# New planning costs, waiting times and an engine-pair rule in a list schedule, with two bias blocks recorded later: attention with relative bias and a mixture of experts on one NeuronCore

## The chip, the cores and the metric

The kernel runs as one program on one core of a Trainium2 chip. The metric is the device time of one execution in microseconds (us). Three runs of the kernel before took 1742.33 to 1742.76 us, with a median of 1742.48 us.

## The reference, cut to what matters

Two stages follow one another. The first is attention over 4 batches, 8 heads, 576 positions and a head size of 64; its scores get a bias from a small network over the distance of two positions. The second is a layer of 8 experts over the 2304 tokens, weighted by a matrix that eight rounds of row and column scaling have balanced.

```python
x = (log1p(abs(i - j)) / log1p(max(i, 1)))[..., None]
bias = relu(x @ w1 + b1) @ w2
attn = softmax(q @ k.T / sqrt(D) + bias) @ v
P = exp(x @ w_gate - max);  8 times: rows, then columns of P scaled
out = sum over e of P[:, e:e+1] * (relu(x @ m1[e]) @ m2[e])
```

## The kernel before, in words

Both stages are first written down as a list of nodes and then emitted in an order that a list scheduler works out when the program is built. On the chip each engine runs its instructions in just that order, and semaphores hold an instruction until its inputs are there. So the scheduler's numbers set the order of each queue and nothing else: they add no wait and take none away.

**The planner.** `Plan` (lines 44 to 171) holds the nodes. `Engine` (line 190) stands in for an engine: every call such as `vec.tensor_tensor(...)` becomes a node with a planned duration from `cost` (line 227), or for a DMA from `transfer` (line 215). `emit` (line 131) walks through planned time. For each engine it takes, of the nodes that are ready, the one with the lowest priority number and then the lowest index, which is the order in which the code recorded it (`pick`, line 144). Priority 0 is `urgent` (line 87), 2 is `later` (line 94), the rest are 1. A successor becomes ready at the planned end of a node plus an entry of `LATENCY` (line 48), or 0.17 us where the table has none. At the end all nodes are sorted by planned start and issued. The one table `LATENCY` serves both stages, while `cost` serves the attention alone: the experts' nodes carry durations that are written out by hand (`on_act`, `on_vec`, `on_pe`).

**The start.** The 16 blocks of q and k are loaded, and VectorE or ScalarE takes the largest magnitude of each. Beside that run the bias blocks: `bias_step` (line 624) issues `bias_front(i)` (line 544: one DMA of a mask for block i+3, four matmuls, four ScalarE sign operations) and `bias_back(i-1)` (line 558: two groups of 17 matmuls on TensorE and two or three VectorE operations). There are 41 blocks. Two of them follow each of eight pairs of maxima (lines 803 and 804). Then the maxima are turned into the scale of q and k by a chain under `urgent`: a reduction, a transpose on TensorE, a reduction, a small matmul, and a few VectorE operations. From block 18 on `bias_back` needs a factor that comes from this scale.

**The attention.** 16 units of two heads each go through: cutting q and k into high and low fp16 halves (`u_cut`, line 707), transposes, scores (`scores`, line 898, two PSUM buffers `s`), the maximum with the bias added (`st_max`, line 922, a VectorE instruction of 576 columns with an accumulated result, called CUSTOM_DVE_ANT_0 in the profile), the exponential with its sum (`st_exp`, line 940, ScalarE), the cut of the probabilities into a high half (`st_hi`, line 956, ScalarE) and a low half (`st_lo`, line 969, VectorE), a DMA transpose into `aT`, and the product with v (`attend`, line 983: a group of 28 matmuls into PSUM buffer `pv`, with 64 partitions each, of 256 columns in 32 groups and of 64 columns in 16). GpSimd copies halves of tiles from one set of partitions to the other. Expert 0's first products are fed in as pieces of 12 matmuls with priority 2 (`run_piece`, line 868) once the first tokens are there. All the attention's instructions have line 211 in the profile, the helper that records them.

**The experts.** Line 1191 emits the attention's plan, line 1927 that of the experts, which are seven experts of Strassen-like products on TensorE (lines 1608 and 1628 in the profile) with their evacuations on ScalarE and VectorE.

In the old `cost`, a VectorE operation is 0.12 us and 1.2 ns (SBUF) or 1.12 ns (PSUM) for each column; a ScalarE operation is 0.16 us (0.13 from PSUM), 0.03 us for each single-column operand and 0.97 ns for each column, with 0.28 us more where it accumulates.

Of the kernel before, what the change touches and what calls it, by code (L numbers as in the profile page):

```python
# [10 lines left out]
F32 = mybir.dt.float32  # L11
# [4 lines left out]
PSUM = bass.MemoryType.PSUM  # L16
# [19 lines left out]
SK = 3.0  # L36
PC = 1.305
MXP = 2
K_VEC = (1, 4, 7)
TM16 = 2.0**-16  # L40
TINY = 2.0**-100
# [2 lines left out]
class Plan:  # L44
# [1 line left out]


    LATENCY = {
        ("act", "act"): 0.13,
        ("dve", "dve"): 0.13,  # L50
        ("pool", "pool"): 0.1,
        ("pe", "pe"): 0.0,
        ("sp", "sp"): 0.0,
        ("dve", "pe"): 0.26,
        ("pe", "act"): 0.2,
        ("pe", "dve"): 0.2,
    }

    def record(self, eng, cost, fn, ins, outs, move=None):
# [71 lines left out]
    def emit(self):  # L131
        n = self.nodes
        succ, left, ready = [[] for _ in n], [len(x[3]) for x in n], [0.0] * len(n)
        for i, x in enumerate(n):
            for d in x[3]:
                succ[d].append(i)
        avail = {}
        for i, x in enumerate(n):
            if not left[i]:
                avail.setdefault(x[0], []).append(i)  # L140
        free, order, moved = {}, [], 0.0
        key = lambda i: (n[i][4], i)

        def pick(e):

            l = avail[e]
            t = max(free.get(e, 0.0), min(ready[i] for i in l))
            for i in sorted((i for i in l if ready[i] <= t), key=key):
                if not any(n[j][4] == 0 and n[i][4] and t < ready[j] < t + n[i][1] - 0.25 for j in l):
                    return t, e, i  # L150
            t = min(ready[j] for j in l if ready[j] > t)
            return t, e, min((i for i in l if ready[i] <= t), key=key)

        while any(avail.values()):
            t, e, i = min(pick(e) for e in avail if avail[e])
            avail[e].remove(i)
            order.append((t, i))
            free[e] = end = t + n[i][1]
            if n[i][6]:
                moved = max(moved, end + 0.65) + n[i][6][0]  # L160
                end = moved + 0.8
                if e == "dma":
                    free[e] = max(free[e], moved - n[i][6][1])
            for j in succ[i]:
                left[j] -= 1
                ready[j] = max(ready[j], end + n[i][5] + self.LATENCY.get((e, n[j][0]), 0.17))
                if not left[j]:
                    avail.setdefault(n[j][0], []).append(j)
        assert len(order) == len(n)
        for _, i in sorted(order):  # L170
            n[i][2]()
        self.__init__()
# [17 lines left out]
class Engine:  # L190
# [5 lines left out]
    def __getattr__(self, op):  # L196
        def call(*args, **kw):
            outs = [kw[k] for k in ("out", "accum_out") if k in kw]
            rest = list(args)
            if "out" not in kw:  # L200
                outs.insert(0, rest.pop(0))
            ins = [x for x in rest + [v for k, v in kw.items() if k not in ("out", "accum_out")] if isinstance(x, AP)]
            if op == "matmul" and not kw["start"]:
                ins.append(outs[0])
            fn = getattr(self.real, op)
            move = None
            if op.startswith("dma"):
                cost, *move = self.transfer(op, outs[0], ins[0])
            else:
                cost = self.cost(op, outs[0], ins) + (0.28 if self.name == "act" and len(outs) > 1 else 0.0)  # L210
            self.plan.record(self.name, cost, lambda: fn(*args, **kw), ins, outs, move)  # L211

        return call
# [13 lines left out]
    def cost(self, op, out, ins):  # L227

        n = max(x.free_size() for x in [out] + ins)
        columns = sum(x.free_size() == 1 for x in ins)  # L230
        if self.name == "pe":
            c = 4 if ins[0].dtype == F32 else 1
            if out.partition_size() > 64:
                return c * max(64, out.free_size()) / 2350
            return c * max(82, out.free_size()) / 3500
        if self.name == "act":
            return (0.13 if ins and ins[0].space == PSUM else 0.16) + 0.03 * columns + n * 0.00097
        if self.name == "pool":
            return 0.15 + n * 0.0016
        if op == "tensor_copy" and ins[0].dtype == out.dtype == F16:  # L240
            return 0.06 + n * 0.00027
        if n <= 2:
            return 0.08
        return 0.12 + n * (0.0012 if ins[0].space != PSUM else 0.00112)


class Places:
# [24 lines left out]
def attention_sinkhorn_moe(ctx, tc, q, k, v, w1, b1, w2, wg, m1, m2, xm, xm4, xf, sel, out):  # L272
# [12 lines left out]
    vec, act, pool, pe, sync = (  # L285
        Engine(plan, e, n)
        for e, n in ((nc.vector, "dve"), (nc.scalar, "act"), (nc.gpsimd, "pool"), (nc.tensor, "pe"), (nc.sync, "dma"))
    )
# [47 lines left out]
    def some_max(o, i, on_act):  # L336

        if on_act:
            act.activation(i, i, AF.Abs, accum_out=o)
        else:  # L340
            absmax(o, i)
# [72 lines left out]
    with ExitStack() as actx:  # L414
# [24 lines left out]
        big, hidp, scon = Places(take, 4), Places(take, 2), Places(take)  # L439
# [50 lines left out]
        def max_load(name, src, i):  # L490
            flat = src.rearrange("b h s d -> (b h s d)").rearrange("(n p x) -> n p x", p=P, x=1152)
            if name == "v":
                f = (wrk if i % 2 else bst).tile([P, 1152], F32, name="mxl", tag="aT" if i % 2 else "bt", bufs=2 + i % 2)
            else:
                f = big.tile([P, 1152], F32, name="big")
            sync.dma_start(out=f, in_=flat[i])
            mxt[name, i] = f
# [22 lines left out]
        for kind in range(1, 4):  # L520
            vec.scalar_tensor_tensor(
                out=wr,
# [8 lines left out]
            out=wa.rearrange("p g (j k) -> p (g j) k", j=4),  # L531
            in0=wr.unsqueeze(1).broadcast_to([P, 16, HID]),
            in1=selt[:, 8:24].unsqueeze(2).broadcast_to([P, 16, HID]),
            op=ALU.mult,
# [9 lines left out]
        def bias_front(i):  # L544
            t, s0, n = blk(i)
            W = 8 * n
            xm_load(i + 3)
            if i % 9 == 3 and t < 4:
                xg_load(t + 1)
            x = xq.pop(i)  # L550
            sg = hidp.tile([P, 4, 512], F16, name="sg", tag="sg")
            for g4 in range(4):
                pre = ps_l1() if g4 % 2 else psA.tile([P, 512], F32, name="pre", tag=("pv", "l2")[g4 // 2])
                pe.matmul(pre[:, :W], wa[:XR, g4], x, start=True, stop=True)
                act.activation(sg[:, g4, :W], pre[:, :W], AF.Sign)
            sgs[i] = sg
# [67 lines left out]
        def bias_step(between=()):  # L624

            i = bpos[0]
            bpos[0] += 1
            if between:
                if 0 < i <= NBLK:
                    bias_back(i - 1)  # L630
                for j, fn in enumerate(between):
                    fn()
                    if j == 0 and i < NBLK:
                        bias_front(i)
                return
            if i < NBLK:
                bias_front(i)
            if 0 < i <= NBLK:
                bias_back(i - 1)
# [12 lines left out]
            out=w1r, in0=pw[:, H : H + 2], scalar1=s_wb[:, 0:1], scalar2=2.0**-11, op0=ALU.mult, op1=ALU.mult  # L652
# [5 lines left out]
            out=w2m,  # L658
            in0=w2r.unsqueeze(2).broadcast_to([P, H, 4]),
            in1=selt[:, 4:8].unsqueeze(1).broadcast_to([P, H, 4]),  # L660
            op=ALU.mult,
# [131 lines left out]
        for n in range(8):  # L793
            for m in (2 * n, 2 * n + 1):
                nm, _, i = qk_order[m]
                some_max(mq8[:, int(nm == "k"), i : i + 1], mxt.pop((nm, i)), nm == "k" and i not in K_VEC)
                if m + 4 < 16:
                    max_load(*qk_order[m + 4])
                elif m + 4 == 16:
                    u_load(0)  # L800
                if m + 4 >= 16:
                    max_load("v", v, m - 12)
            bias_step()
            bias_step()
        with plan.urgent():
            mqk = sm([P, 2])
            vec.tensor_reduce(out=mqk, in_=mq8, axis=AX.X, op=ALU.max)
# [4 lines left out]
            out=c8, in0=u_qk[:, 0:1], scalar=0.125, in1=u_qk[:, 1:2], op0=ALU.mult, op1=ALU.mult  # L812
# [7 lines left out]
            out=g, in0=g0, scalar=s_qk[:, 0:1], in1=s_qk[:, 1:2], op0=ALU.mult, op1=ALU.mult  # L820
        )
        gbox[0] = g[:, 0:1]
        bias_step()

        def b_scale(hp):

# [21 lines left out]
            u_trans(0)  # L848
        u_load(1)
        u_cut(1)  # L850
        bias_step()
        b_scale(0)
        u_trans(1)

# [258 lines left out]
        for u in range(len(units)):  # L1113
            f = 5 * u
            g1 = 8 + 3 * u if u < 4 else f + 2
            e = 0 if u < 4 else -1
# [75 lines left out]
        vec, act, pool, pe, sync = nc.vector, nc.scalar, nc.gpsimd, nc.tensor, nc.sync  # L1192
# [289 lines left out]
    def w_max(e, w):  # L1482
        prio = 0 if e == 1 else MXP
        for i, q in enumerate(BLK):
# [413 lines left out]
    for n, (e, b) in enumerate(seq):  # L1898
        r = visit[n]
        i, at_end, leaves = (b, r % 2), n % 5 == 4, visit[n + 1 : n + 2] != [r]  # L1900
# [96 lines left out]
```

## Time and profile before

| what | value |
|---|---|
| median of three runs | 1742.48 us (1742.33 to 1742.76) |
| the profiled execution's own time | 1743.0 us |
| span of its trace | 1741.2 us |
| TensorE busy, share of the span | 1667.7 us, 96% |
| VectorE busy | 1440.8 us, 83% |
| ScalarE busy | 1070.2 us, 61% |
| GpSimd busy | 96.8 us, 6% |
| mean granted TensorE clock | 0.984 of full |

PE is TensorE's matmuls, PEld its weight loads, DVE VectorE, ACT ScalarE, POOL GpSimd and SP the queue that issues DMAs. Busy time is the union of the instructions of an engine. Two instructions that follow one another on DVE or ACT overlap a little in the trace, so what one of them costs its engine is the time from its start to the start of the next, which is less than its duration. The attention runs from 0 to about 492 us, the experts from there to the end.

### The profile page before, as it was taken

What the parts mean: (1) busy time and instruction counts of PE and PEld (TensorE: products, weight loads), DVE (VectorE), ACT (ScalarE), POOL (GpSimd) and SP (SyncE); (2) the same over time, 40 slices, a digit from 0 to 9 for tenths busy, and PEclk for the clock granted to TensorE, in tenths of its full rate; (3) what the DMA queues carried; (4) which work ended last, traced back from release to release, by engine and by line L of the source; (5) the groups of instructions that cost most, each with busy time, mean ns of one, the idle gap of its engine ahead of it and who ended that gap; (6) DMA issues with size and microseconds to landing.
All of it is one profiled execution on the core that took longest, in us unless ns stands there. A gap on an engine that the chain in (4) does not pass through costs nothing.

```text
span 1741.2 us, 40333 instructions
## 1 busy us (share of the span) xinstructions
PE 1667.7 (96%) x16596; PEld 1368.3 (79%) x16596; DVE 1440.8 (83%) x2622; ACT 1070.2 (61%) x1906; POOL 96.8 (6%) x137
## 2 busy tenths in 40 slices
PE   7887897999999999999999999999999999999998
PEld 4554564656585888888988898889888888888887
DVE  7998989898869999787878887988788878876666
ACT  7897888888857655456455545555555644443443
POOL 0102011111002310000000000000000000000000
PEclk9988898999999999999999999999999999999999
DMA  7869899999976446734664555456544743463321
GB/s 256 257 172 235 190 211 208 215 203 208 185 228 212 148 164 230 247 145 147 218 231 170 174 187 212 173 177 237 208 163 158 281 155 133 181 224 99 102 76 37
DMA packets 291965, 324.61 MB, mean 186 GB/s; under 512 B 183100, under 2 KB 217412, under 8 KB 286788
## 3 DMA queue, kind: packets, MB, share of 16 engines
q1 hardware_dynamic: 291780, 322.04, 61.0%
q8 instruction: 129, 2.11, 0.5%
q14 instruction: 56, 0.46, 0.1%
HBM read 191.43 MB, written 88.08 MB: 161 GB/s over the span
## 4 chain that ended last, share of the span: by engine, by line
PE 81%; DVE 9%; DMA 4%; ACT 3%; issue 2%; POOL 0%; SPq 0%; DVEq 0%; ACTq 0%; POOLq 0%
PE bankA L1608 18%; PE bankA L1628 14%; PE bankE L1628 9%; PE bankB L1628 9%; PE bankE L1608 9%; PE l L211 7%; PE s L211 5%; PE bankB L1608 4%; PE pv L211 3%; DMA aT<-ah 2%; ACT area L211 1%; DVE area L211 1%; DVE ah L211 1%; DMA aT<-xc 1%; PE bankB L375 1%
## 5 line engine op out<-in xcount | busy, mean ns | idle before, releaser
L1608 PEld LDWEIGHTS <-slot 128*128 128x128 f16 x5040 | 451.0, 98 | 51.1 <-issue 5.3
L1628 PEld LDWEIGHTS <-hA 128*128 128x128 f16 x2268 | 221.0, 98 | 26.6 <-DVE hA L1220 1.2
L211 PEld LDWEIGHTS <-area 128*128 128x128 f16 (+1 forms) x2477 | 153.8, 100 | 102.8 <-issue 33.1
L1608 PE MATMUL bankA<-xt,slot 128*128 128x256 f16 (+1 forms) x1680 | 186.1, 262 | 0.7 <-ACT u L1665 0.7
L1608 PE MATMUL bankE<-xt,slot 128*128 128x256 f16 (+1 forms) x1680 | 186.1, 262 | 0.3 <-DVE c L1220 0.3
L1653 ACT ACTIVATE hA<-c 128x512 f16<-128x512 f32 x189 | 118.3, 628 | 108.5 <-DVE c L1220 107.5
L1628 PEld LDWEIGHTS <-hS 128*128 128x128 f16 x1512 | 147.5, 98 | 20.2 <-DVE hS L1659 1.9
L1628 PEld LDWEIGHTS <-area 128*128 128x128 f16 x1512 | 147.7, 98 | 17.1
L1712 ACT COPY u<-bankA 128x512 f32<-128x512 f32 (+1 forms) x70 | 37.9, 541 | 178.9 <-PE bankA L1628 178.8
L1220 DVE SCALAR_TENSOR_TENSOR hA<-c,hA 128x512 f16<-128x512 f32 x189 | 128.3, 690 | 16.0 <-ACT hA L1653 13.9
L1665 ACT ACTIVATE u<-bankA 128x512 f32<-128x512 f32 x126 | 75.1, 596 | 79.0 <-PE bankA L1608 71.9
L211 PE MATMUL l<-area 128*128 128x512 f16 (+1 forms) x413 | 110.0, 384 | 5.5 <-ACT area L211 1.3
L211 ACT ACTIVATE sb<-sb,st 128x576 f32<-128x576 f32 x144 | 110.6, 770 | 7.1 <-DVE st L211 6.8
L1220 DVE SCALAR_TENSOR_TENSOR acc<-c,fs,acc 128x256 f32<-128x256 f32 x252 | 110.3, 479 | 2.0
L211 DVE SCALAR_TENSOR_TENSOR ah<-sb,st,ah 128x576 f16<-128x576 f32 x121 | 97.5, 828 | 13.4 <-ACT ah L211 13.4
L211 PE MATMUL s<-qkT 128*128 128x512 f16 (+3 forms) x560 | 83.0, 297 | 15.5 <-DVE st L211 14.4
L211 ACT ACTIVATE ah<-sb,st 128x576 f16<-128x576 f32 x121 | 89.4, 771 | 11.6 <-DMA aT<-ah 9.6
L1628 PE MATMUL bankA<-area,hS 128*128 128x256 f16 x756 | 88.9, 273 | 1.8 <-ACT hS L1653 1.0
L1628 PE MATMUL bankA<-area,hA 128*128 128x256 f16 x756 | 88.4, 273 | 1.0 <-DVE hA L1220 1.0
L1628 PE MATMUL bankB<-area 128*128 128x256 f16 x756 | 88.3, 273 | 0.0
L1628 PE MATMUL bankB<-area,hA 128*128 128x256 f16 x756 | 88.3, 273 | 0.0
L1628 PE MATMUL bankA<-area 128*128 128x256 f16 x756 | 88.3, 273 | 0.0
(248 smaller groups left out, 3166.7 us busy)
## 6 DMA issues: line engine op xcount, KB each, us to landing
sc_w<-stage SPq DMA_DIRECT2D x84, 512.0 KB
acc<-sc_y SPq DMA_DIRECT2D x102, 256.0 KB
area<-sc_w SPq DMA_DIRECT2D x48, 512.0 KB
sc_y<-acc SPq DMA_DIRECT2D x84, 256.0 KB
xt<-sc_t SPq DMA_DIRECT2D x20, 1024.0 KB
slot<-sc_w SPq DMA_DIRECT2D x36, 512.0 KB
bt<-sc_bias SPq DMA_DIRECT2D x26, 576.0 KB
raw<-in_moe_w_dram SPq DMA_DIRECT2D x28, 512.0 KB
```

The costliest lines, as they stand in the source:

```text
L211: self.plan.record(self.name, cost, lambda: fn(*args, **kw), ins, outs, move)
L375: pe.matmul(ps, w[:, a, ft * P : (ft + 1) * P], xs(xp, dt, p0, W), start=(dt == 0 and j == 0), stop=(dt == 3 and j == 2),)
L1220: vec.scalar_tensor_tensor(out=o, in0=x, scalar=s, in1=y, op0=op0, op1=op1)
L1608: pe.matmul(ps[:, jf * w : jf * w + w], t[:, a, c * 512 + f * P : c * 512 + f * P + P], x(xp, c), start=(first and jf == 0 and c == 0 and ...
L1628: pe.matmul(ps[:, j * 256 : j * 256 + 256], h[:, a, fc * w + j * P : fc * w + j * P + P], t[:, wp, fc * 256 : fc * 256 + 256], start=(firs ...
L1653: on_act(0.58, lambda: act.activation(h[:, 0, sl], x, AF.Relu if relu else AF.Copy), [r], wk)
L1665: on_act(0.55, lambda: act.activation(tmp[k], bank[b], f, scale=HS), [b], [k], 0)
L1712: on_act(0.27 * nt, lambda: act.copy(tmp[k][:, :n], bank[b][:, :n]), [b], [k], 0)
```

## The change

The planner's numbers are replaced and three things are added to it. `LATENCY` gets new entries. `cost` gets new figures for every engine. An accumulating ScalarE operation is given 0.093 us more instead of 0.28. VectorE operations that read two tensors of SBUF, or copy or scale one from SBUF to SBUF, are marked "shared"; in planned time such an operation and a GpSimd operation no longer overlap: whichever was chosen later starts when the other has ended. The choice of node in `pick` does not look at that mark, and the sort at the end uses the start from before the shift. No semaphore comes with it.

In the bias blocks, the two `bias_step` calls after the eighth pair of maxima are left out, and one call behind the scale becomes three (`EARLY`). The call after the second cut of q and k stays (4 - EARLY is 1). So blocks 15 and 16 are recorded behind the scale's chain instead of ahead of it. What is computed doesn't change.

```diff
+EARLY = 3
...
     LATENCY = {
-        ("act", "act"): 0.13,
-        ("dve", "dve"): 0.13,
-        ("pool", "pool"): 0.1,
+        ("act", "act"): 0.055,
+        ("act", "dve"): 0.225,
+        ("act", "pe"): 0.225,
+        ("dve", "dve"): 0.06,
+        ("dve", "act"): 0.2,
+        ("dve", "pe"): 0.2,
+        ("pool", "pool"): 0.0,
+        ("pool", "dve"): 0.12,
+        ("pool", "pe"): 0.12,
         ("pe", "pe"): 0.0,
+        ("pe", "act"): 0.29,
+        ("pe", "dve"): 0.29,
         ("sp", "sp"): 0.0,
-        ("dve", "pe"): 0.26,
-        ("pe", "act"): 0.2,
-        ("pe", "dve"): 0.2,
     }
...
             order.append((t, i))
+            if e == "pool" or n[i][6] == "shared":
+                t = max(t, free.get(("shared", e != "pool"), 0.0))
+                free["shared", e == "pool"] = t + n[i][1]
             free[e] = end = t + n[i][1]
-            if n[i][6]:
+            if n[i][6] and n[i][6] != "shared":
...
             move = None
+            big = [x for x in ins if x.free_size() > 1]
+            if self.name == "dve" and not any(x.space == PSUM for x in big):
+                one = len(big) == 1 and op in ("tensor_scalar", "tensor_copy", "tensor_single_scalar")
+                move = "shared" if len(big) > 1 or one and outs[0].free_size() > 1 else None
...
-                cost = self.cost(op, outs[0], ins) + (0.28 if self.name == "act" and len(outs) > 1 else 0.0)
+                cost = self.cost(op, outs[0], ins) + (0.093 if self.name == "act" and len(outs) > 1 else 0.0)
...
         n = max(x.free_size() for x in [out] + ins)
-        columns = sum(x.free_size() == 1 for x in ins)
+        full = [x for x in ins if x.free_size() > 1]
+        psum = any(x.space == PSUM for x in full)
         if self.name == "pe":
-            c = 4 if ins[0].dtype == F32 else 1
-            if out.partition_size() > 64:
-                return c * max(64, out.free_size()) / 2350
-            return c * max(82, out.free_size()) / 3500
+            c = (4 if ins[0].dtype == F32 else 1) * max(64, out.free_size()) / 2375
+            return c if out.partition_size() > 64 else c / 2
         if self.name == "act":
-            return (0.13 if ins and ins[0].space == PSUM else 0.16) + 0.03 * columns + n * 0.00097
+            return (0.052 if psum else 0.186) + n * 0.00083
         if self.name == "pool":
-            return 0.15 + n * 0.0016
+            return 0.08 + n * (0.00115 if len(full) < 2 else 0.0025)
+        if n <= 2:
+            return 0.072
         if op == "tensor_copy" and ins[0].dtype == out.dtype == F16:
-            return 0.06 + n * 0.00027
-        if n <= 2:
-            return 0.08
-        return 0.12 + n * (0.0012 if ins[0].space != PSUM else 0.00112)
+            return 0.065 + n * (0.00053 if psum else 0.00027)
+        return 0.065 + n * 0.00106 + (0.05 if not psum and len(full) > 1 else 0.0)
...
                     max_load("v", v, m - 12)
-            bias_step()
-            bias_step()
+            if n < 7:
+                bias_step()
+                bias_step()
...
         gbox[0] = g[:, 0:1]
-        bias_step()
+        for _ in range(EARLY):
+            bias_step()
...
         u_cut(1)
-        bias_step()
+        for _ in range(4 - EARLY):
+            bias_step()
```

## Rows read from the trace of the kernel before

**Rows 1.** Busy time by stretch: width, PE, PEld, DVE, ACT, POOL, clock, DMA share, GB/s

```profile
0.00:20.00 20.00, 10.76 (x68) 5.51 (x69) 11.12 (x34) 8.85 (x16) 1.81 (x11) 1.00 0.66 220
20.00:60.00 40.00, 37.61 (x593) 24.04 (x592) 35.90 (x52) 35.21 (x70) 0.00 (x0) 1.00 0.90 290
60.00:200.00 140.00, 113.77 (x1362) 69.63 (x1361) 131.36 (x275) 118.77 (x229) 19.02 (x35) 0.88 0.83 212
200.00:260.00 60.00, 57.74 (x590) 37.21 (x588) 52.47 (x121) 51.44 (x107) 7.58 (x12) 1.00 0.93 195
260.00:320.00 60.00, 47.07 (x494) 29.55 (x493) 55.16 (x128) 51.03 (x105) 9.30 (x15) 0.89 0.99 209
320.00:492.00 172.00, 164.70 (x1653) 107.81 (x1652) 144.74 (x336) 143.66 (x294) 20.05 (x32) 1.00 0.99 205
492.00:1741.00 1249.00, 1236.05 (x11858) 1094.55 (x11851) 1010.09 (x1681) 661.26 (x1091) 39.02 (x34) 1.00 0.50 176
```

**Rows 2.** Waits, 0 to 492 us: engine, tile, what for, us, times, longest

```profile
PE s L211 <- DVE st L211: 18.5, 22, 2.1
DVE ah L211 <- ACT ah L211: 13.4, 16, 2.2
DVE sms L211 <- DMA area<-in_moe_w_dram: 1.4, 1, 1.4
```

**Rows 3.** Timeline, ACT: start, duration, instruction

```profile
28.88 1.57 ACT L211 ACTIVATE area<-l 128x512 f16<-128x512 f32 x3
...
332.96 0.77 ACT L211 ACTIVATE sb<-sb,st 128x576 f32<-128x576 f32 x1
...
333.72 1.43 ACT L211 ACTIVATE xc<-sb,st 128x576 f16<-128x576 f32 x2
```

**Rows 4.** Groups by form, ACT, 0 to 492 us: count, busy us, mean ns, idle before

```profile
L211 ACT ACTIVATE sb<-sb,st 128x576 f32<-128x576 f32 x144 | 110.6, 770 | 7.1 <-DVE st L211 6.8
L211 ACT ACTIVATE area<-l 128x512 f16<-128x512 f32 x120 | 65.1, 627 | 4.5 <-PE l L211 4.2
```

**Rows 5.** Timeline, DVE

```profile
341.03 1.54 DVE L211 SCALAR_TENSOR_TENSOR ah<-sb,st,ah 128x576 f16<-128x576 f32 x2
...
343.91 0.80 DVE L211 CUSTOM_DVE_ANT_0 sb<-s,br,sms 128x576 f32<-128x576 f32 x1
...
344.64 0.81 DVE L211 CUSTOM_DVE_ANT_0 sb<-s,br,sms 128x576 f32<-128x576 f32 x1
```

**Rows 6.** Timeline, PE: two groups of the product with v

```profile
336.71 1.96 PE L211 MATMUL pv<-aT,vs 128*64 128x256 f16 x28
...
341.33 0.86 PE L211 MATMUL pv<-aT,vs 128*64 128x64 f16 x28
```

**Rows 7.** Chain of waits, 260 to 320 us

```profile
297.19 6.10 DMA aT<-xc
```

**Rows 8.** Timeline: GpSimd's copies and a VectorE operation beside them

```profile
148.26 3.00 POOL L211 COPY br<-area 64x512 f32<-64x512 f32 x4 [0.76 <-DVE area L211]
...
148.87 1.26 DVE L211 SCALAR_TENSOR_TENSOR ah<-sb,st,ah 128x576 f16<-128x576 f32 x1
```

**Rows 9.** Groups by form, DVE, 0 to 492 us: the low halves

```profile
L211 DVE SCALAR_TENSOR_TENSOR ah<-sb,st,ah 128x576 f16<-128x576 f32 x121 | 97.5, 828 | 13.4 <-ACT ah L211 13.4
```

**Rows 10.** Timeline: the scale's reduction, transpose and first use

```profile
47.52 0.17 DVE L211 TENSOR_REDUCE sms<-sms 128x2 f32<-128x16 f32 x1
...
55.55 0.27 PE L211 MATMUL l<-ident,sms 128*2 128x128 f32 x1
...
59.66 0.78 ACT L211 ACTIVATE qk<-nat,sms 128x576 f16<-128x576 f32 x1
```

**Rows 11.** Waits of PE, 492 to 1741 us: the longest in total

```profile
PE bankA L1608 <- ACT u L1665: 3.5, 4, 1.3
```

**Rows 12.** Waits of ACT, 0 to 492 us: for the product with v

```profile
ACT xb L211 <- PE pv L211: 7.1, 6, 2.8
ACT xc L211 <- PE pv L211: 6.2, 9, 1.4
```

## The prediction

> **What bounds the kernel now.** I read the busy time by stretch first [rows 1]. Its idle time says where anything can be won: the width less PE's busy time. From 492 us on, in the experts, PE idles 13.0 of 1249 us. In the attention it idles 9.2 us before 20 us, 2.4 from 20 to 60, 26.2 from 60 to 200, 2.3 from 200 to 260, 12.9 from 260 to 320 and 7.3 from there to 492. So there are two kinds of stretches. From 60 to 200 and from 260 to 320 VectorE sets the pace: it is busy 131.4 of 140 and 55.2 of 60 us, and its idle time is 8.6 and 4.8 us. From 200 to 260 and from 320 to 492 PE does, at 96%, fed with expert 0's pieces. PE's lower granted clock, 0.88 and 0.89 of full, stands just in VectorE's two stretches: those are means of the two levels, 2.4 and 1.2 GHz, and PE idled 19% and 22% of these stretches. A clock that stays up there helps VectorE only through shorter waits.
>
> The waits come second [rows 2]. PE's longest is for the maximum to empty a score buffer, 18.5 us: PE waiting on the pacing engine. VectorE waits 13.4 us for ScalarE's high halves, which is mere order, and 1.4 us for a weight load, which is a DMA's lateness.
>
> **The costs that the plan believed.** A wrong duration costs nothing by itself; it puts instructions in the wrong order in a queue. ScalarE was furthest off. An exponential with its sum starts the next operation 0.76 us later (332.96 to 333.72), a high half 0.66 us later (1.43 less 0.77), and an operation of 512 columns from PSUM 0.49 us later ((1.57 less a last one of about 0.60) by 2) [rows 3]. The old costs are 1.03, 0.75 and 0.63 us, the new ones 0.76, 0.66 and 0.48. There are 144 exponentials, as many high halves, and 120 signs of the last kind [rows 4]: 144 x 0.27 + 144 x 0.09 + 120 x 0.14 is 69 us, on an engine that is busy 408.9 us in the attention (the sum of its rows to 492). The old plan so took ScalarE for the busiest engine, with more than 470 us of work; the new one has it about right. VectorE moves less: two low halves take 1.54 us, so 0.74 us from start to start (old 0.81, new 0.73), and two maxima start 0.73 us apart (old 0.77, new 0.68) [rows 5].
>
> One edit goes the wrong way. A group of 28 matmuls on v takes up to 1.96 us with 256 columns and up to 0.86 with 64 [rows 6]. The old plan says 28 x 256/3500 = 2.05 and 28 x 82/3500 = 0.66; the new says 28 x 256/2375/2 = 1.51 and 28 x 64/2375/2 = 0.38. So 32 x 0.45 + 16 x 0.48 = 22 us of PE's work at most vanish from the plan.
>
> **What order can win, term by term.** VectorE's stretches hold 13.5 us of its own idle time. It can't go below 0, so that is the ceiling. The floor is a loss, by the 22 us above; its price stands with the second rival. Some of the 13.5 isn't order: the weight load's 1.4 us, and the transposes that land after 6.10 us [rows 7] where the unchanged formula plans 0.65 + 18 x 0.165 + 0.8 = 4.4. I take half, 6.7 us, as the wrong ScalarE costs were large and VectorE's own small. In PE's stretches 9.6 us are idle; with PE at 96% and the underpriced groups there I take a third, 3.2 us (between 0 and 9.6).
>
> **The pair rule.** GpSimd's four copies took 3.00 us, and the low half beside them 1.26 instead of 0.77 us [rows 8]: they do hold each other up. But neither choice nor sort looks at the shift, and no wait is added, so the chip still starts whichever is ready first. The price to be won is small: 121 low halves took 828 ns on average [rows 9], against about 800 for one with nothing beside it (the first of the two in rows 5: 1.54 less 0.74), which is 3.4 us; I double it to 7 for all other paired operations. I take 0, between 7 won and 7 lost, since reordering can as well bring more overlap. The Trainium skill (SBUF — State Buffer, "SBUF: two separate sides") says that the pair is an exclusive lock held for a whole instruction, whoever starts first. By that alone all of GpSimd's 56 us from 20 to 492 us would be closed to paired operations, and the ceiling would be 56 us instead of 7; the 828 ns speak for the small one.
>
> **The two bias blocks.** The scale's reduction is done at 47.7 us, its transpose starts only at 55.55, and the first cut of q at 59.66 [rows 10]: eight us in which PE's queue still had bias blocks ahead. Two of them move behind the chain with all they issue: 8 sign operations (3.9 us of ScalarE at 0.49), their matmuls, their VectorE operations, and two mask loads on SP. Those loads were the last on SP's list before the scale, which issues none, so they pass no other transfer; POOL's queue has nothing there. The chain may come up to 8 us sooner. But the blocks' work is only put off, and VectorE is busy 35.9 of 40 us from 20 to 60: at most 4.1 us of its idle time can be filled, at least 0, and a late mask can take some back. I take 1 us.
>
> **The experts.** Their durations stay, their `LATENCY` does not, so their order may shift by neighbours. PE idles 13.0 of 1249 us there [rows 1], 5 of these at the very end, and its longest wait totals 3.5 us [rows 11]. I take 0, between 5 won and 8 lost (about what is idle now, doubled but for the end).
>
> **Sum.** 6.7 + 3.2 + 0 + 1.0 + 0 = 10.9 us off the profiled execution's 1743.0 us, which lies 0.5 above the median of the runs. Against the median: **1731.6 us**.
>
> **The rivals.** *No change that can be measured.* VectorE and PE still have the same work; new orders bring new waits in place of old ones, and terms of +3 and -3 cancel: 1742.5 us. For it: VectorE already runs at 94% from 60 to 200 us. Against it: 69 us of error on one engine.
>
> *Slower, by the underpriced groups.* Planned 0.45 us too short, their evacuations stand too early on ScalarE, ahead of exponentials that are ready. ScalarE waits 13.3 us for such groups now [rows 12]. With all 22 us added and half passed on to VectorE (ScalarE's idle time from 20 to 492 us, 71.9 us, takes the rest), less 4 us won elsewhere, it is +7: 1749.5 us. It decides where those waits rise over some 30 us.
>
> *Slower, by VectorE's start.* If a VectorE operation began only when the one before had ended, each of 288 maxima and low halves would be planned 0.1 us too short (0.81 against 0.70), 29 us in all, and by the same half +10: 1752.5 us. The rows speak against it: the second maximum starts 0.07 us before the first ends [rows 5]. [...]
>
> *Much faster.* Both of VectorE's stretches close up (13.5), half of PE's idle goes (4.8), and the doubled lock price is won (7): 25 us, 1717 us. For it: fewer waits also keep PE's clock up. Against: the DMA-led waits stay.
>
> **How the numbers follow.** Forecast 0.50, between 1726 and 1738.8; much faster 0.09; no change 0.17; underpriced groups 0.20; VectorE's start 0.04. About 0.2% (3.5 us) is what a measurement of this kernel can tell from no change. So faster 0.59, same 0.17, slower 0.24. The range reaches from the much faster case to the first slower one, 1716 to 1750 us; it leaves out the tails of both, less than 2 in 10.
>
> **What would show it.** Right: VectorE's idle time from 60 to 320 us falls, its wait for ScalarE's high halves falls below 13.4 us, the experts start some 10 us before 492 us and take as long as now; the transpose of the scale starts within 3 us of its reduction. The count and length of instructions stay; low halves stay near 828 ns. Wrong: ScalarE's waits for the groups on v over 30 us, the experts' stretch longer than 1249 us, or transposes that land later and hold PE.

## The result, and the profile after

The changed kernel takes 1760.68 us (median of four runs, 1758.50 to 1763.99) against 1742.62 for the kernel before beside it (four runs, 1742.33 to 1746.03). The ratio is 1.0101, with a 95% interval of 1.0078 to 1.0123: slower by 17.6 us where 11 us less were forecast, and outside the range. The profiled execution took 1758.97 us with a span of 1757.2, 16.0 longer than before. TensorE runs the same 16596 matmuls and is busy 1664.8 us (1667.7 before), so the 16 us are idle time: it idles 92.4 us of the span, 18.9 more than before.

This is the busy time by stretch of the kernel after: width, PE, PEld, DVE, ACT, POOL, clock, DMA share, GB/s. The attention now ends at 502 us, so the last two stretches are 182 and 1255 us wide.

```profile
0.00:20.00 20.00, 11.26 (x89) 6.03 (x89) 9.94 (x34) 8.32 (x15) 1.80 (x11) 1.00 0.54 186
20.00:60.00 40.00, 35.45 (x534) 21.49 (x531) 34.78 (x52) 33.05 (x65) 0.00 (x0) 1.00 0.87 283
60.00:200.00 140.00, 110.02 (x1367) 67.55 (x1366) 131.13 (x267) 117.38 (x230) 20.66 (x35) 0.90 0.84 210
200.00:260.00 60.00, 58.08 (x586) 38.04 (x586) 53.62 (x128) 53.53 (x110) 4.77 (x7) 0.95 0.86 188
260.00:320.00 60.00, 45.78 (x490) 27.73 (x489) 54.83 (x128) 52.52 (x107) 10.72 (x15) 0.97 1.00 205
320.00:502.00 182.00, 169.36 (x1706) 109.19 (x1705) 145.70 (x337) 145.49 (x294) 20.70 (x35) 1.00 0.96 203
502.00:1757.00 1255.00, 1234.83 (x11841) 1093.45 (x11837) 1010.94 (x1681) 659.29 (x1091) 32.44 (x34) 1.00 0.50 175
```

Width less PE's busy time, stretch by stretch against [rows 1]: PE idles 2.2 us more from 20 to 60, 3.8 more from 60 to 200, 1.3 more from 260 to 320, 5.3 more from there to the end of the attention, and 7 more in the experts. VectorE's idle time, where 6.7 us were to be won, is 8.9 and 5.2 us in its two stretches, as before (8.6 and 4.8). The same view from 0 to 320 us in one piece shows how far each engine had come. First the kernel before, then the kernel after:

```profile
0.00:320.00 320.00, 266.94 (x3101) 165.93 (x3102) 286.02 (x606) 265.29 (x523) 37.71 (x72) 0.93 0.88 218
```

```profile
0.00:320.00 320.00, 260.59 (x3059) 160.84 (x3060) 284.30 (x605) 264.79 (x523) 37.95 (x68) 0.94 0.86 212
```

VectorE (605 instructions for 606) and ScalarE (523 for 523) are level at 320 us. TensorE is 42 matmuls and 6.4 us of busy time behind. By their groups, 28 of these are one group on v of 64 columns and 14 are pieces of expert 0, about 2.8 us of work that has to be done later; the rest of the 6.4 us is the same matmuls in less time (192 pieces `l<-xa,area` took 23.0 us for 25.0).

The waits of the kernel after, 0 to 502 us (engine, tile, what for, us, times, longest), those that answer to [rows 2] and [rows 12] and those that grew:

```profile
ACT sb L224 <- DVE st L224: 26.1, 38, 2.5
PE s L224 <- DVE st L224: 26.0, 26, 4.7
DVE ah L224 <- ACT ah L224: 22.0, 23, 3.9
...
PE l L224 <- DVE sms L224: 11.0, 5, 5.1
...
ACT xc L224 <- PE pv L224: 6.7, 9, 1.4
...
ACT xa L224 <- PE pv L224: 4.0, 8, 1.7
...
ACT xb L224 <- PE pv L224: 1.6, 2, 1.2
```

PE's wait for the maximum rose from 18.5 to 26.0, VectorE's for the high halves from 13.4 to 22.0; ScalarE's wait for maxima was 6.8 us before. Its waits for the groups on v, by which the slower rival was to be known above 30 us, fell from 13.3 to 8.3 in the two tiles of [rows 12]. A third tile, `xa`, takes such groups too; with it they fell from 17.5 to 12.3. PE's wait for `sms` in the kernel before was this:

```profile
PE l L211 <- DVE sms L211: 4.4, 5, 1.3
```

PE's waits for the maximum and for `sms` are the two that count: 7.5 and 6.6 us more, while all its other waits together are 2.4 less. That makes the 11.7 us that PE idles more up to the experts' first gate matmul (72.0 us for 60.4). It is busy 2.2 us less there, so the experts begin 9.5 us later (502.19 less 492.65). Both rises are clear of what one order shows from one execution to the next: in three other traces of the order of before (e2, e9 and e16 below) the wait for the maximum is 19.7 to 20.4 us and that for `sms` 3.5 to 4.2. Of the 11.7 us, 6.4 lie before 320 us and 5.3, in many small waits, behind it.

PE's wait for `sms` is one place. Behind the start, `sms` holds the scales of the gate's and the experts' weights, which are reduced on VectorE, transposed on PE and multiplied out. Their transposes in the timeline on PE, first of the kernel before, then of the kernel after; in brackets the idle time ahead:

```profile
167.56 0.27 PE L211 MATMUL l<-ident,sms 128*2 128x128 f32 x1 [1.23 <-DVE sms L211]
...
169.92 0.27 PE L211 MATMUL l<-ident,sms 128*1 128x128 f32 x1 [0.41 <-DVE sms L211]
```

```profile
166.21 0.37 PE L224 MATMUL l<-ident,sms 128*2 128x128 f32 x1 [4.32 <-DVE sms L224]
...
173.59 0.37 PE L224 MATMUL l<-ident,sms 128*1 128x128 f32 x1 [5.09 <-DVE sms L224]
```

PE stands in front of a transpose whose reduction VectorE hasn't done. With the two small matmuls behind them, these waits are 10.4 us from 60 us on, against 3.7 in the kernel before: 6.7 us more. One rule of `pick` that the account of the planner leaves out may bear on it: on an engine where an `urgent` node will soon be ready, no other node is started that would delay it by more than 0.25 us, and the transposes of the scales are urgent. A plan that expects them too soon then has nothing in front of them; that it went so here was not looked up in the plan.

The very end of the attention looks like a third place, and isn't one. There the chain that ended last runs through a DMA transpose:

```profile
490.88 1.02 PE l L224 x8
491.90 4.80 DMA aT<-ah
496.74 1.93 PE pv L224 x27
```

A chain names at each step only what released the next one. What PE did meanwhile stands in its timeline, first of the kernel before, then of the kernel after:

```profile
481.74 5.29 PE L211 MATMUL l<-xc,area 128*128 128x256 f16 x47 [0.60 <-DVE xc L211]
```

```profile
490.88 5.29 PE L224 MATMUL l<-xc,area 128*128 128x256 f16 x47 [0.55 <-DVE xc L224]
...
496.74 1.93 PE L224 MATMUL pv<-aT,vs 128*64 128x256 f16 x27 [0.35 <-DMA aT<-ah]
```

In both kernels PE works through 47 matmuls there. In the kernel after the transpose lands just behind them, and 0.35 us is all that PE idles for it.

From their first gate matmul to the end of the span the experts then take 6.4 us longer, 1255.0 us for 1248.6.

### The profile page after: what moved, and what is told of

Read it like the earlier page. It is cut to its first block, busy times and chain, and to the rows that moved or that the text cites. A ratio compares the mean times of both kernels' runs of the same rounds, so it can differ in the third digit from the quotient of the medians.

```text
span 1757.2 us, 40306 instructions
## 1 busy us (share of the span) xinstructions
PE 1664.8 (95%) x16596; PEld 1363.5 (78%) x16596; DVE 1440.9 (82%) x2622; ACT 1069.6 (61%) x1906; POOL 91.1 (5%) x137
## 4 chain that ended last, share of the span: by engine, by line
PE 80%; DVE 10%; ACT 4%; issue 2%; DMA 2%; POOL 0%; SPq 0%; ACTq 0%; DVEq 0%; POOLq 0%
PE bankA L1623 18%; PE bankA L1643 14%; PE bankE L1643 9%; PE bankB L1643 9%; PE bankE L1623 9%; PE l L224 7%; PE bankB L1623 4%; PE s L224 4%; PE pv L224 3%; DVE sb L224 2%; ACT area L224 1%; DVE ah L224 1%; DVE area L224 1%; DVE sms L224 1%; PE bankB L387 1%
## 5 line engine op out<-in xcount | busy, mean ns | idle before, releaser
L1623 PEld LDWEIGHTS <-slot 128*128 128x128 f16 x5040 | 450.9, 98 | 56.5 <-issue 10.4
L1643 PE MATMUL bankE<-area,hS 128*128 128x256 f16 x756 | 88.5, 273 | 2.2 <-ACT hS L1668 1.8
```

The costliest lines, as they stand in the source:

```text
L1623: pe.matmul(ps[:, jf * w : jf * w + w], t[:, a, c * 512 + f * P : c * 512 + f * P + P], x(xp, c), start=(first and jf == 0 and c == 0 and ...
L1643: pe.matmul(ps[:, j * 256 : j * 256 + 256], h[:, a, fc * w + j * P : fc * w + j * P + P], t[:, wp, fc * 256 : fc * 256 + 256], start=(firs ...
```

## The experiments

Each row of the table stands beside runs of the kernel before on the same chip; us is the ratio's excess times 1743 us. The last column is the first gate matmul of the experts in the one profiled trace.

| run | edit | ratio (95%) | us | gate at |
|---|---|---|---|---|
| after | all | 1.0101 (1.0078 to 1.0123) | +17.6 | 502.19 |
| e1 | after, experts on the old table | 1.0073 (1.0058 to 1.0088) | +12.7 | 503.60 |
| e2 | before, experts on the new table | 1.0045 (1.0030 to 1.0060) | +7.8 | 496.65 |
| e9 | e2, entries between engines only | 1.0032 (1.0022 to 1.0042) | +5.6 | 496.03 |
| e16 | before, experts with 0.1 us between engines | 1.0030 (1.0017 to 1.0043) | +5.2 | 491.35 |
| e4 | ScalarE's durations | 1.0046 (1.0031 to 1.0061) | +8.0 | 500.60 |
| e5 | new table in the attention | 1.0027 (1.0017 to 1.0037) | +4.7 | 494.80 |
| e6 | VectorE's durations | 1.0075 (1.0052 to 1.0098) | +13.1 | 507.05 |
| e7 | TensorE's durations | 1.0081 (1.0060 to 1.0101) | +14.1 | 507.83 |
| e8 | pair rule | 1.0007 (0.9995 to 1.0020) | +1.2 | 496.92 |
| e3 | bias blocks | 0.9993 (0.9977 to 1.0008) | -1.2 | 493.13 |
| e11 | e7, groups on v as measured | 0.9997 (0.9985 to 1.0008) | -0.5 | 494.76 |
| e10 | e1, groups on v as measured | 1.0019 (1.0009 to 1.0028) | +3.3 | 494.05 |
| e13 | e6, maxima 0.05 us longer | 1.0070 (1.0054 to 1.0086) | +12.2 | 507.01 |
| e14 | e10, maxima 0.05 us longer | 1.0041 (1.0025 to 1.0058) | +7.1 | 501.92 |
| e17 | e4 and e6 | 1.0047 (1.0030 to 1.0064) | +8.2 | 498.82 |
| e12 | VectorE 0.01 us longer | 1.0032 (1.0018 to 1.0046) | +5.6 | 497.81 |
| e15 | VectorE 0.01 us shorter | 1.0010 (0.9997 to 1.0023) | +1.7 | 493.86 |
| e18 | e3 and e11 | 1.0034 (1.0024 to 1.0044) | +5.9 | 499.70 |

The attention's order is one and the same in before, e2, e9 and e16, and yet its experts begin at 492.65, 496.65, 496.03 and 491.35 us. So a single trace places the attention's end only to some 5 us; verdicts rest on the ratios, and traces serve for mechanisms. The experts' own length is steadier: from the first gate matmul to the end of the span it is 1246.8 to 1250.9 us in all sixteen traces whose experts have the old table.

**Which stage lost?** e1 puts the old table back behind the attention's `emit`; e2 does the reverse (the tables themselves are left out here).

```diff
     plan.emit()
+    plan.LATENCY = Plan.OLD    # e1, on the changed kernel
+    plan.LATENCY = Plan.NEW    # e2, on the kernel before
```

> The changed kernel, but the experts' plan gets the old table of waiting times back; the attention's plan stays new. Theory (two separate losses: some 9.5 us in the attention's order, some 6.5 us in the experts' order by the table they share): the experts take 1248.5 us from their first gate matmul again, and the whole about 1754 us. Rival (the experts' loss is carried over from the attention's later end, or is noise of their transfers): no change, about 1760 us.

> The kernel before, with the new table of waiting times in the experts' plan alone. Theory (the table alone costs the experts some 6.5 us): 1749 us, the attention ends at 492 us as before. Rival (carried over from the attention): 1742.5 us.

e1 took 4.9 us of the 17.6 away (the two intervals overlap), and its experts run 1248.5 us (span 1752.1 less 503.60) as before. e2 added 7.8, and its experts run 1253.9. The traces with the new waits between engines in the experts have 1255.0 (after), 1253.9 (e2) and 1254.4 us (e9), all outside the 1246.8 to 1250.9 of the old table. So the table that serves both stages costs 5 to 8 us in the experts, and the attention loses the remaining 12.7. PE's waits in the experts name a place; here is the longest in total of e2:

```profile
PE bankA L1625 <- ACT u L1682: 7.1, 10, 0.7
```

It was 3.5 us in 4 times [rows 11], so 3.6 us of the 5.3 that the experts take longer in e2's trace; in the kernel after it is 7.8 in 11. The timeline shows one of them on PE, of the kernel before and of e2 at the same place:

```profile
881.77 1.47 PE L1608 MATMUL bankA<-xc,area 128*128 128x256 f16 x12
883.08 2.78 PE L1628 MATMUL bankA<-area,hA 128*128 128x256 f16 x24
885.70 2.78 PE L1628 MATMUL bankE<-area,hA 128*128 128x256 f16 x24
888.32 1.47 PE L1608 MATMUL bankA<-xc,slot 128*128 128x256 f16 x12
```

```profile
887.37 1.47 PE L1625 MATMUL bankA<-xc,area 128*128 128x256 f16 x12
889.58 1.47 PE L1625 MATMUL bankA<-xc,slot 128*128 128x256 f16 x12 [0.74 <-ACT u L1682]
890.89 2.78 PE L1645 MATMUL bankE<-area,hA 128*128 128x256 f16 x24
```

Before, second-layer products (`hA`) stood between two first-layer products in bank A, 5.24 us in which ScalarE could drain the bank. In e2 the second one comes at once, and waits 0.74 us for that drain (whether the `hA` product behind it was ready to go ahead, the trace doesn't show). e9 and e16 ask which entries do it. e9 takes the new entries between engines (0.12 to 0.29 us) and leaves the old ones on an engine; e16 makes all waits between engines 0.1 us.

> The kernel before; in the experts' plan alone the waiting times from one engine to another are new, those within an engine old. Theory (the experts' hand-written durations already reach to the end of an instruction, so longer waits from engine to engine count that end twice, and second-layer products that are ready look late): about 1750 us, experts near 1254 us, TensorE's waits for ScalarE at the first product of a layer about 7 us in all instead of 3.5. Rival (the shorter waits within ScalarE and VectorE do it): 1743 us, experts at 1249 us.

> The kernel before; in the experts' plan alone every waiting time from one engine to another is 0.1 us. Theory (the hand-written durations there already reach to an instruction's end, so short waits are the right ones): the experts take no longer than before, 1244 to 1249 us, TensorE's waits for ScalarE at most 3.5 us, whole 1739 to 1743 us. Rival (the old table is best by trial, a step to either side costs): 1746 to 1752 us.

e9 has most of e2's loss, and its wait for `u` is 9.1 us, so most of it comes from the entries between engines. My reading was that the experts' written durations already hold an instruction's end, so that the added wait counts it twice. It fell with e16: with short waits the experts still took 1252.3 us, and the wait for `u` was 6.5 us. Both longer and shorter waits lose; why the old table's mix is better stays open.

**Which part cost the attention its 12.7 us?** Each part but one was made alone on the kernel before (GpSimd's new figures in `cost` were not, and stay untested): e4 the ScalarE lines of `cost` with the 0.093, e5 the table, e6 the VectorE lines, e7 the TensorE lines, e8 the pair rule, e3 the bias blocks, all as in the diff of the change (e5 goes back to the old table before the experts).

> The kernel before, with the new ScalarE durations alone in the attention's plan. As the prediction had it (ScalarE's durations were the large error, and mending them tightens the order): 5 to 10 us faster, 1733 to 1738 us. Rival (the 69 us too much on ScalarE were slack that kept orders robust, and taking it away makes ScalarE's queue wait for VectorE): 5 to 10 us slower, about 1750 us.

> The kernel before, with the new table of waiting times in the attention's plan alone, experts old. Theory (waits of 0.05 to 0.1 us shift neighbours only): within 3 us of 1742.5. Rival (the table carries the attention's loss): 1752 us, the attention ends near 502 us.

> The kernel before, with the new VectorE durations alone in the attention's plan. Theory (a plan that believes VectorE, the pacing engine, to be faster than it is runs the other engines' queues ahead of it): 3 to 10 us slower. Rival (the durations are nearer to the trace's starts, so the order is no worse): within 3 us of 1743, or faster.

> The kernel before, with the new TensorE durations alone in the attention's plan. Theory of the prediction's slower rival (groups on v planned 22 us too short at most): ScalarE's waits for these groups grow over 30 us and the run is about 7 us slower. Rival (TensorE's queue is not what the order hangs on): within 3 us of 1743.

> The kernel before, with only the rule for VectorE's SBUF pairs and GpSimd. Theory (bookkeeping that adds no wait): within 3 us of 1743, low halves at 820 to 835 ns as before. Rival (it does keep the two apart): low halves near 800 ns and some 3 to 7 us faster.

> The kernel before, with only the two bias blocks behind the scale. As the prediction had it: the scale's transpose starts within 3 us of its reduction and the run is 0 to 3 us faster. Rival (the blocks were work that filled the scale's chain, and now stand in the way of the first units): 2 to 5 us slower.

The pair rule and the bias blocks can't be told from nothing. Each of the four sets of numbers loses: 8.0 + 4.7 + 13.1 + 14.1 is 40 us, three times what they cost together, so they don't add. Nor does a price that is nearer to the rows help by itself: e4, the term on which the forecast stood, loses 8 us where 5 to 10 won were expected. e5, e6 and e7 lost more than was expected of them too (3, 10 and 7 us at most). In e4 ScalarE's exponentials wait for their maxima:

```profile
ACT sb L211 <- DVE st L211: 29.3, 33, 2.5
```

It was 6.8 us before. That wait isn't the loss itself: e10 has 22.9 us of it with 3.3 us lost, and e17 21.7 with 8.2 lost.

**The groups on v.** e11 and e10 give the group its measured time, (columns + 64)/2375/2 for a matmul into at most 64 partitions. That plans 28 of them at 1.89 and 0.75 us for 256 and 64 columns; the change has 1.51 and 0.38, the rows up to 1.96 and 0.86 [rows 6]. e11 has the rest of e7, e10 the rest of e1. The same line prices the scores' last 64 positions and the scales' transposes, some 2 us of planned work beside 18 us for the groups; these were not tried apart. And its prices lie near the old ones (2.05 and 0.66 us), so e11 can't tell a right price from the old one.

```diff
-            c = (4 if ins[0].dtype == F32 else 1) * max(64, out.free_size()) / 2375
+            n = out.free_size() + (64 if out.partition_size() <= 64 else 0)
+            c = (4 if ins[0].dtype == F32 else 1) * max(64, n) / 2375
             return c if out.partition_size() > 64 else c / 2
```

> The kernel before with TensorE's new durations alone, but the groups on v priced as measured. Theory (it was the underpricing): 1741 to 1746 us instead of 1758.8. Rival (any move away from the old numbers costs some 10 us): 1750 to 1760 us.

> The changed kernel with the experts on the old table and the groups on v priced as measured ((columns + 64) at 2375 per us, halved: 1.89 and 0.75 us for 28 matmuls). Theory (the underpriced groups are most of the attention's loss, as the run with TensorE's durations alone suggests): 1740 to 1746 us. Rival (any plan of shorter durations loses, whichever is right): 1753 to 1758 us, as with the groups underpriced.

Two lines took 14.6 us off one kernel and 9.4 off the other, both beyond their intervals. The traces agree: these are the busy times from 0 to 320 us of e7, e11 and e10.

```profile
0.00:320.00 320.00, 258.73 (x2974) 160.87 (x2975) 275.62 (x582) 253.55 (x499) 38.30 (x68) 0.91 0.85 210
```

```profile
0.00:320.00 320.00, 266.78 (x3108) 167.27 (x3108) 283.60 (x606) 263.65 (x523) 36.66 (x72) 0.93 0.88 218
```

```profile
0.00:320.00 320.00, 267.11 (x3100) 163.99 (x3101) 285.89 (x609) 265.23 (x526) 38.44 (x69) 0.93 0.86 213
```

e7 is 127 matmuls and 24 VectorE instructions behind the kernel before, e11 is level, and e10 has back what the kernel after lacks. Both waits of the result shrink in e10. PE's waits for the maximum and, from 60 us on, for `sms`, first in e1, then in e10:

```profile
PE s L235 <- DVE st L235: 25.2, 25, 4.7
PE l L235 <- DVE sms L235: 11.5, 4, 5.4
```

```profile
PE s L235 <- DVE st L235: 21.1, 22, 2.9
PE l L235 <- DVE sms L235: 5.7, 4, 2.5
```

4.1 and 5.8 are 9.9 us of the 11.8 that PE idles less there, and e10's experts begin 9.6 us sooner than e1's. In e7 the short price bites elsewhere: in VectorE's wait for scores, from 200 to 330 us, first before, then e7:

```profile
DVE sb L211 <- PE s L211: 1.5, 4, 0.7
```

```profile
DVE sb L211 <- PE s L211: 8.4, 8, 2.1
```

So one short price shows as different waits in two plans. A reading that fits is that the plan takes PE to be free sooner than it is, and that what is placed behind that belief comes out wrong wherever it is tight. This is argued, not shown: the plans were not compared step by step, and e14 (below), which has the groups as measured, has both waits again:

```profile
PE s L235 <- DVE st L235: 24.3, 27, 5.7
PE l L235 <- DVE sms L235: 9.0, 4, 4.7
```

**How rough is the ground?** e12 and e15 change VectorE's 0.12 us to 0.13 and 0.11. e13 and e14 give the maxima (`tensor_tensor_reduce`) 0.05 us more, to 0.73 us, what they take from start to start [rows 5]; e17 has ScalarE's and VectorE's durations together, e18 the two harmless parts.

```diff
-        return 0.12 + n * (0.0012 if ins[0].space != PSUM else 0.00112)
+        return 0.13 + n * (0.0012 if ins[0].space != PSUM else 0.00112)
```

> A control: the kernel before with 0.01 us added to each planned VectorE duration in the attention, which is further from the trace and far too small to matter for what is late. Theory (single wrong prices explain the losses): within 3 us of 1743. Rival (the old numbers were a point found by trial in rugged ground, and any step off it costs): 5 to 12 us slower.

> The other control: the kernel before with 0.01 us taken from each planned VectorE duration in the attention, a step towards the trace. Theory (the ground is rugged, the sign of a small step doesn't matter): 3 to 12 us slower, like the control that adds 0.01. Rival (too long is what costs): within 3 us of 1743 or faster.

> The kernel before with VectorE's new durations alone, but the maximum priced at its measured 0.73 us instead of 0.68. Theory (the pacing engine's one underpriced operation, 144 x 0.05 = 7 us, makes the loss of the run with VectorE's durations alone): at most 6 us slower than before, under 1749 us. Rival (it is the ground: any step off the old numbers costs some 6 to 15 us): 1749 to 1758 us.

> The changed kernel, experts on the old table, groups on v and the maximum both priced as measured: the plan nearest to the trace. Theory (prices nearer to the trace give a better order): under 1743 us, faster than the 1746.9 of the run with the groups alone mended. Rival (what is left is the ground): 1743 to 1751 us, no better.

> The kernel before with the new durations of ScalarE and of VectorE together. Theory (what counts is how the two stand to each other: VectorE priced down alone leaves ScalarE overpriced by 69 us): 1743 to 1749 us, less than either alone (1750.8 and 1757.9). Rival (each brings its own loss and they add): 1757 to 1768 us.

> The kernel before with the two parts that alone cost nothing: the two bias blocks behind the scale, and TensorE's durations with the groups on v as measured. Theory (a version that could beat both kernels): 1739 to 1743 us. Rival (two harmless steps together are one more step off the old numbers): 1745 to 1752 us.

A hundredth of a microsecond more, which is far too small to matter for what is late, costs 5.6 us; a hundredth less (e15) can't be told from nothing, against the 3 to 12 us expected. e18 costs 5.9 though neither part costs anything. A right price for the maxima changes e6 by nothing its interval would show (12.2 for 13.1) and makes e10 worse (7.1 for 3.3), where a run under 1743 us was expected. So a loss of some 6 us can't be put down to any one number, and the losses of e4 and e5 and what is left of e10 stay open. The 14.6 us between e7 and e11 are well beyond that measure. The 9.4 between e1 and e10 are beyond it too, but e14 leaves open how much of them is the price and how much the order that it happened to give. e6's 13 us are beyond that measure, but what in VectorE's figures does it wasn't found: the maxima are not it, and with ScalarE's figures beside them (e17) the loss is 8.2 (the two intervals overlap, and 1743 to 1749 us were expected for 1750.7). No run here beats the kernel before; e3, e8, e11 and e15 can't be told from it.

## Why the prediction was wrong

- **"I take half, 6.7 us, as the wrong ScalarE costs were large"** is the step that failed, and it failed in sign. The prices were read rightly, and better prices on ScalarE alone lost 8.0 us (e4), 14.7 from the 6.7 won that the step stood for. The step held that a truer duration gives a better order. The runs don't bear that out: VectorE's idle time stayed (8.9 and 5.2 us), e4, e6 and e17 all lost, and e14, the plan nearest to the rows, lost 7.1. Why ScalarE's truer prices lose is open. The 3.2 us for PE's stretches went the same way: PE idled 5.3 us more from 320 us on.
- **The underpriced groups** were a rival at 0.20, and their price is the largest single part that the runs show: 14.6 us alone (e7 to e11), 9.4 in the whole change (e1 to e10, with what e14 leaves open). The rival had the sign, not the size (7 us) and not the sign to look for. ScalarE's waits for the groups, `xa` with them, fell to 12.3 us instead of passing 30. They are 22.0 in e7, which loses 14.1 us, and 23.5 in e11, which loses nothing, so they don't tell the two apart. What rose in the kernel after is PE's own waits, for maxima and for the weights' scales. "Half passed on to VectorE" had looked at the evacuations only.
- **The experts, "I take 0, between 5 won and 8 lost"**: the upper end held. They lost 6.4 us in the trace and 5 to 8 by e1 and e2, more than half of it in PE's longest wait, which came 11 times instead of 4. The range should have carried these 8 us on top of the rival's 7: both ends together, 15 us, come near the 17.6 measured.
- **Its signs of being wrong**: one came (the experts' stretch got longer), the waits for the groups did not pass 30 us, and transposes did not hold PE: its waits for `aT` were 6.0 us before and 1.6 after.
- **Much faster** had for it that fewer waits keep PE's clock up. The kernel after shows more idle time with a higher clock: in VectorE's two stretches PE idles 3.8 and 1.3 us more, at a granted clock of 0.90 and 0.97 of full for 0.88 and 0.89, means of its two levels, 1.2 and 2.4 GHz.
- **The pair rule**, taken as 0: right, +1.2 us (e8) within its interval. The low halves stand at 823 ns against 828 [rows 9], and at 825 in e8. This is their group in the kernel after; the column before the last is the mean in ns:

```profile
L224 DVE SCALAR_TENSOR_TENSOR ah<-sb,st,ah 128x576 f16<-128x576 f32 x121 | 96.7, 823 | 22.2 <-ACT ah L224 22.0
```

The price was as small as the prediction had it, since few of them meet a copy: by the records of the trace before, 17 of the 121 overlap one of GpSimd's copies and took 929 ns on average, the other 104 took 812, which is 2 us in all. The Trainium skill (SBUF — State Buffer, "SBUF: two separate sides") has the port pair locked for a whole instruction, so that the other side blocks. Six of the 17, at 1.03 to 1.26 us, agree with that; eleven took 0.80 to 0.82, and whether a copy waited there instead, GpSimd's rough spans don't show.

- **The two bias blocks**, 1.0 us: the local step was right, its worth at the end was nothing (e3, 0.9977 to 1.0008). In the timeline of the kernel after, the scale's reduction, its transpose and its first use are

```profile
52.83 0.17 DVE L224 TENSOR_REDUCE sms<-sms 128x2 f32<-128x16 f32 x1
...
53.36 0.27 PE L224 MATMUL l<-ident,sms 128*2 128x128 f32 x1
...
56.13 1.44 ACT L224 ACTIVATE qk<-nat,sms 128x576 f16<-128x576 f32 x2 [0.86 <-DVE sms L224]
```

The transpose follows 0.5 us after the reduction (8.0 before, [rows 10]; "within 3 us" was predicted), and the first cut comes 3.5 us sooner though the reduction came 5.3 later. In e3 the cut comes 4.6 us sooner, at 55.04, and the lead is gone by the end of the attention, as "the blocks' work is only put off" said.
- **VectorE's start**, the second slower rival: the duration it asked for the maxima was tried in the size that the rows give (e13, e14) and helped nowhere. Its full 0.1 us, for the low halves too, was not tried.

## What to carry to other kernels

In a list schedule a price only sets an order, so a truer one need not give a faster kernel. Change one engine's prices at a time, look for every other plan that shares the table, and look at what the engine of the underpriced work waits for, not only at what evacuates it. Hold a wait that a chain shows against the timeline of the engine: 4.80 us in the chain were 0.35 us of idle time here. Beside each new plan time a neutral step (here 0.01 us on one engine): what that loses is the least that a verdict on one number must exceed.

## What the chip showed that was not expected

- A matmul into 64 partitions costs more than half a full one of the same columns: a group of 28 of 256 columns takes 1.89 us in the last chain of e7 and e11, 0.135 us a pair, while twelve full ones start the next run 1.31 us later (881.77 to 883.08), 0.109 each.
- One order of the attention, run in four kernels, ended between 491.35 and 496.65 us, more than most of the effects that were looked for; whole executions scatter as much (1740.10 to 1747.12 us for the kernel before in one set of 20), and only their medians agree far better (1741.99 to 1743.72 us over the five sets of runs).
